# A conditioned transformer block with windowed attention: first modulation from two PSUM banks each, one load for the later modulation columns, a new order on all engines

## The chip, the cores and the metric

The kernel runs on one core of a Trainium2 chip. Five instruction queues work side by side: PE (TensorE, matrix multiplication), DVE (VectorE), ACT (ScalarE), POOL (GpSimd) and SP (SyncE, which here only issues DMA transfers). Each engine takes its own instructions strictly in the order in which the program lists them; between engines there are semaphore waits. The metric is the device time of one execution in microseconds (us), lower is better.

## The reference

One layer: a layer norm whose scale and shift come from a condition vector `c`, attention with a dilated window, a gated residual, and the same again around a two-layer network. All tensors are bf16; S is 2048 tokens, D is 448, there are 16 heads of 28, and F is 1792.

```python
mod = (silu(c) @ w_mod).reshape(1, 6, 1, 448)
sa, ca, ga, sb, cb, gb = (mod[:, i] for i in range(6))
h = layernorm(x) * (1 + ca) + sa
x = x + ga * A(h)              # qkv = h @ wqkv ; window of 8 keys, dilation 2
h = layernorm(x) * (1 + cb) + sb   # ; softmax ; @ wo
x = x + gb * (silu(h @ w1) @ w2)
```

In `A`, token s sees the keys s, s-2, ..., s-14, so even and odd tokens never mix.

## The kernel before

The 2048 tokens are worked in four chunks of 512 (k = 0 to 3), each as 2 x 256 even and odd tokens. Attention runs in nine blocks of about 112 tokens per parity (b = 0 to 8), the two-layer network in the same four chunks. The steps, with the lines of the kernel before:

- `Norm` (L468 to L578) makes the normalized tokens `xn`: statistics by bn_stats on DVE (L480) or by two passes on ACT (L484, L490), a power on POOL (L496), the normalization (L506 to L510). Its result is transposed either on PE, for the first chunk only (`on_pe`, L536, transposes at L546), or by a DMA on SP's queue (`on_dma`, L565, L568). After the transpose the scale and shift of `modc` are applied, the modulation: L552 on ACT or L554 on DVE for the first chunk, L573 or L575 for the others.
- `project` (L639) makes q and k (matmuls at L648, copies out of PSUM at L652) and v (L668, copies at L661). The weights of q and k are first copied into a padded layout (`pad`, L581 to L586, "wp" in the profile).
- `logits` and `values` (L680, L740): q times k at L696, exponent on ACT at L704, mask on DVE at L728, attention times v at L754, normalization on DVE (L759, L760), and a transposing DMA on SP's queue (L764).
- `out_proj` (L775): matmuls at L784, residual add on DVE at L787.
- `ffn1` and `ffn2` (L800, L822): matmuls at L811, silu on ACT at L819, matmuls at L831, residual add on DVE at L836, store at L839.
- The condition: `mod_cols` (L434) makes the scale and shift columns with 32 small matmuls (L444) and copies them into `modc` (L447, L448); `gate` (L454) makes the two gates with four matmuls each (L460), which are then multiplied into the weights (L860, L863).
- `warm_up` (L414) feeds PE with 19 matmuls of no use (7, and six pairs) while the first data are on their way.

Projections use `phases` (L589): each group of 14 matmuls is a "straight" half of 8 and a "crossed" half of 6, which other work may come between.

The order of everything is written out by hand: `ORDER` (L43) lists the numbers of all operations, with the PSUM banks that each takes behind a slash (a "big" number is a pair of banks, a "one" number a single bank) and with v or a where a step can run on DVE or on ACT. `Plan.emit` (L204) emits the instructions in that order, which fixes each engine's queue. The durations, rates and due times beside the operations feed a search for such an order and are not used when `ORDER` is given.

In the first chunk, `on_pe` puts the four transposed 128-column pieces of one half of the tokens (i = 0, 1) into one PSUM bank, and four operations per half modulate one piece each.

The modulation weights `w_mod` lie in `both` and come in eight loads: two for the first norm's columns (issued first on SP), then two each for the first gate, for the second norm, and for the second gate (`load_mod`, L373 and L384).

Of the kernel before, what the change touches and what calls it, by code (L numbers as in the profile page):

```python
# [7 lines left out]
BF16 = mybir.dt.bfloat16  # L8
# [7 lines left out]
D = 448  # L16
H = 16
DH = 28
F = 1792
# [59 lines left out]
def half(j):  # L79
    return slice(K3 * j, K3 * j + K3)  # L80
# [156 lines left out]
def layer(ctx, tc, io, safe):  # L237
# [96 lines left out]
    for r, n in (("big", 3), ("one", 2), ("v", NV), ("p", NP), ("xn", NX), ("o0", 2), ("o1", 2), ("out", len(outb))):  # L334
        P.resource(r, n)
# [631 lines left out]
```

## Time and profile before

| what | value |
|---|---|
| median of three runs | 174.26 us |
| lowest and highest run | 173.8 and 175.14 us |
| the profiled execution's own time | 173.79 us |
| its span, first to last instruction | 172.1 us |
| DVE busy | 101.5 us (59%) |
| ACT busy | 114.7 us (67%) |
| POOL busy | 15.9 us (9%) |
| moved by DMA | 17.48 MB, 102 GB/s in the mean |

The profiled execution took 1.69 us more than its span, and 0.47 us less than the median. Busy time of PE is modelled where matmuls overlap in its pipeline, so a busy PE isn't always a PE at its best pace. The profile also gives the granted clock of PE for any stretch.

### The profile page before, as it was taken

The numbers are of one execution on the slowest core, as the hardware profiler recorded it, in microseconds if no ns is written. First come the engines' busy times: TensorE is split into PE (matmuls) and PEld (weight loads), VectorE is DVE, ScalarE is ACT, GpSimd is POOL, SyncE is SP. The second block draws the span as 40 slices with busy tenths as digits, with TensorE's granted clock in tenths as the row PEclk, the third lists the DMA queues.
The fourth block names the chain that finished last, engine by engine and source line by source line (L and its number), as shares of the span: only waits on it lengthen the run. The fifth ranks groups of instructions, "written<-read, shape, count | busy, mean of one in ns | idle before, by whom it ended". The sixth has DMA issues, their size and how long they took to land.

```text
span 172.1 us, 4285 instructions
## 1 busy us (share of the span) xinstructions
PE 162.7 (95%) x1762; PEld 82.3 (48%) x1763; DVE 101.5 (59%) x261; ACT 114.7 (67%) x162; POOL 15.9 (9%) x38
## 2 busy tenths in 40 slices
PE   7979999699999999999999999999999999999990
PEld 2524444364465455554456555655444454445540
DVE  6889994998798786655578027897662213001031
ACT  3579999786989876789988679653169850473000
POOL 5411230100000130102000000003001100000000
PEclk9999999996999999999999999999999999999999
DMA  5993799943756725021202002224600501000121
GB/s 193 334 363 83 176 231 260 293 116 75 179 155 132 233 65 114 4 47 33 47 27 84 2 0 57 55 55 93 163 29 6 119 0 59 0 0 4 57 84 36
DMA packets 33347, 17.48 MB, mean 102 GB/s; under 512 B 24296, under 2 KB 32936, under 8 KB 33320
## 3 DMA queue, kind: packets, MB, share of 16 engines
q1 hardware_dynamic: 33168, 16.90, 36.9%
q8 instruction: 16, 0.26, 0.7%
q10 hardware_dynamic: 152, 0.23, 0.4%
q14 instruction: 11, 0.09, 0.2%
HBM read 9.12 MB, written 1.84 MB: 64 GB/s over the span
## 4 chain that ended last, share of the span: by engine, by line
PE 72%; DVE 10%; DMA 7%; ACT 6%; issue 2%; DVEq 0%
PE psum L831 25%; PE psum L811 25%; PE psum L648 7%; PE psum L784 7%; PE psum L754 4%; DMA wqk<-xn 3%; PE psum L696 3%; DMA oT<-o 2%; DMA x_all<-in_A_x_dram 2%; PE psum L668 2%; ACT h L552 2%; DVE p L728 1%; DVE st L480 1%; DVE o L760 1%; PE psum L444 1%
## 5 line engine op out<-in xcount | busy, mean ns | idle before, releaser
L831 PE MATMUL psum<-w,both 128*128 128x448 bf16 x224 | 44.7, 353 | 0.0
L811 PE MATMUL psum<-h,w 64*128 64x512 bf16 x392 | 43.6, 376 | 0.0
L704 ACT ACTIVATE p<-psum 128x896 bf16<-128x896 f32 (+1 forms) x36 | 31.8, 931 | 6.2 <-PE psum L696 3.6
L819 ACT ACTIVATE both<-psum 128x1024 bf16<-128x1024 f32 x28 | 27.3, 1021 | 12.7 <-PE psum L811 12.7
L811 PEld LDWEIGHTS <-w 64*128 64x128 bf16 x392 | 20.8, 94 | 20.9 <-issue 0.5
L831 PEld LDWEIGHTS <-both 128*128 128x128 bf16 x224 | 20.8, 98 | 20.0 <-issue 1.2
L836 DVE TENSOR_TENSOR ot<-psum,x_all 128x448 bf16<-128x448 f32 x16 | 9.8, 621 | 27.5 <-PE psum L831 26.3
L496 POOL TENSOR_TENSOR rs<-rs,negh 128x2 f32<-128x2 f32 x16 | 12.6, 790 | 117.6 <-DVE rs L493 117.4
L648 PE MATMUL psum<-h,wp 64*128 64x512 bf16 x168 | 19.8, 377 | 0.1
L728 DVE TENSOR_TENSOR p<-p,maskb 128x1792 bf16<-128x1792 bf16 (+1 forms) x18 | 19.5, 1099 | 0.6 <-ACT p L704 0.4
L648 PEld LDWEIGHTS <-wp 64*128 64x128 bf16 x224 | 10.7, 97 | 13.2 <-issue 1.7
L490 ACT ACTIVATE screp<-x_all,mv 128x448 bf16<-128x448 bf16 x16 | 10.7, 668 | 7.2 <-DVE mv L487 6.9
L784 PE MATMUL psum<-wo,oT 64*128 64x448 bf16 x112 | 12.7, 350 | 0.2 <-DMA oT<-o 0.2
L668 PE MATMUL psum<-wv,h 64*128 64x448 bf16 x98 | 11.8, 350 | 0.9 <-DVE h L554 0.6
L652 ACT CAST qk<-psum 128x1024 bf16<-128x1024 f32 x11 | 10.8, 1004 | 1.8 <-PE psum L648 1.8
L760 DVE TENSOR_TENSOR o<-psum,rc 112x448 bf16<-112x448 f32 (+1 forms) x18 | 11.2, 624 | 0.6
L787 DVE SCALAR_TENSOR_TENSOR x_all<-psum,x_all 128x448 bf16<-128x448 f32 x16 | 9.4, 621 | 2.7 <-PE psum L784 2.0
L754 PEld LDWEIGHTS <-p 128*128 128x128 bf16 x288 | 8.5, 96 | 4.0 <-issue 1.6
L575 DVE TENSOR_SCALAR h<-h,modc 128x512 bf16<-128x512 bf16 x18 | 6.6, 409 | 6.4 <-DMA h<-xn 6.4
L759 DVE RECIPROCAL rc<-psum 112x16 f32<-112x16 f32 (+1 forms) x18 | 4.5, 252 | 9.8 <-PE psum L754 9.8
L754 PE MATMUL psum<-v,p 128*128 128x29 bf16 x288 | 9.6, 176 | 0.4 <-DVE p L728 0.4
L573 ACT ACTIVATE h<-h,modc 128x512 bf16<-128x512 bf16 x6 | 4.7, 808 | 6.9 <-DMA h<-xn 6.9
(84 smaller groups left out, 142.7 us busy)
## 6 DMA issues: line engine op xcount, KB each, us to landing
out_dram<-ot SPq DMA_DIRECT2D x16, 112.0 KB, 1.8
both<-in_w_mod_dram SPq DMA_DIRECT2D x2, 672.0 KB, 4.8
x_all<-in_A_x_dram SPq DMA_DIRECT2D x3, 448.0 KB, 5.9
w<-in_B_w_dram SPq DMA_DIRECT2D x3, 448.0 KB, 4.9
w<-in_B_w_dram SPq DMA_DIRECT2D x1, 896.0 KB, 6.8
both<-in_w_mod_dram SPq DMA_DIRECT2D x2, 336.0 KB, 4.6
w<-in_B_w_dram SPq DMA_DIRECT2D x1, 672.0 KB, 5.5
wv<-in_A_wqkv_dram SPq DMA_DIRECT2D x2, 224.0 KB, 5.6
```

What stands on the lines that cost most here:

```text
L496: G.tensor_tensor(out=rs[:, j:j + n], in0=rs[:, j:j + n], in1=negh[:, 0:n], op=ALU.pow)
L648: return T.matmul(ps[:, j, :], lhsT=w.rearrange("p h d -> p (h d)"), rhs=h[rows, :, t, 128:128 + CP], start=start, stop=stop)
L652: copy_on(o)(out=qk[:, :, g, :, s0:s0 + CP], in_=ps.rearrange("p j (t s) -> p j t s", t=2))
L668: T.matmul(ps[:, par, 0:D], lhsT=h[rows, par, t, b0:b0 + 128], rhs=wv[rows, t, :], start=start, stop=stop)
L704: S.activation(out=out_, in_=ps[:, :, 0:4 * nq].rearrange("p j (g q) -> p j g q", q=nq), func=ACTF.Exp, scale=SCALE)
L728: V.tensor_tensor(out=p, in0=p, in1=maskb[:, 1 if b == 0 else 0, 0:nq].unsqueeze(1).to_broadcast([128, H, nq]), op=ALU.mult)
L754: T.matmul(ps[:, h, 0:DH + 1], lhsT=p[:, at:at + 128], rhs=v[:, h, 0:DH + 1], start=True, stop=True)
L760: V.tensor_tensor(out=box["o"][0:nq, off:off + D].rearrange("p (h d) -> p h d", d=DH), in0=ps[0:nq, :, 0:DH], in1=r.unsqueeze(2).to_broadc ...
L784: T.matmul(ps[par][:, 0:D], lhsT=oT[rows, t, par, s0:s0 + 128], rhs=wo[rows, par, t, :], start=start, stop=stop)
L811: return T.matmul(ps[:, j, :], lhsT=w, rhs=h[rows, :, t, :], start=start, stop=stop)
L819: silus[k].append(P.op(("act", 904.0), lambda o, i=i, box=box: S.activation(out=hid[:, k % 2, :, i, :], in_=box["ps"], func=ACTF.Silu), [m ...
L831: T.matmul(box["ps"][:, 0:D], lhsT=hid[:, k % 2, f % 2, f // 2, 128 * j:128 * j + 128], rhs=w2[:, f // 2 + 7 * (f % 2), :], start=(f == 0) ...
```

## The change

Three things change.

1. In `on_pe`, the four transposed pieces of each half go to two separate PSUM banks, two pieces each. One operation now modulates the two pieces of a bank, on one engine. So each half has two modulation operations where it had four, and the two may run on different engines. In the new order DVE takes the two pieces of the first bank of the first half, and ACT the other six pieces.
2. The columns of `w_mod` for both gates and for the second norm come in one call of `load_mod`: one load of 1344 KB and one of 224 KB in place of three of 336, 672 and 336 KB and three of 56, 112 and 56 KB.
3. `ORDER` is another list: the queues of all engines, the choice between DVE and ACT, and the banks are all new. The planner's counts of banks and its DMA durations are also changed; they only matter to the search that made the list.

```diff
 ORDER = (
-    "75/0 1 0 5 8 2 9 3 4 7 102 6 11 25 84 95 76 79 23 21 94 61 62 63 66 64 82 13 15 14 73 103 85/2 96 97 101 67 69 104 12 80 78 105 98 99v 22 106 100v 86 "
-    "10 88/2 108 107 89 109v 111/3 112 110a 113v 116a 114v 115a 26 161 118/2 119 162 122a 123a 24 77 81 19 20 120v 121a 83 137/2 17 18 124 27 92a 140/3 163 "
...
+    "1 2 53 3 67/0 68 70 0 5 8 6 86 9 11 21 4 10 25 26 54 23 24 87 22 13 7 55 61 62 57 94 95 88 58 93 15 76 77/2 78 59 96 97 66 19 89 90 71 69 12 73 56 "
+    "80/2 91v 103/3/4 92v 98 99 64 104 100 81 101v 102v 74 105v 107/5/2 108 17 18 147 27 148 149 154 63 72 106a 29 109a 60 14 110a 84v 150 151 75 20 16 82a "
...
-    for r, n in (("big", 3), ("one", 2), ("v", NV), ("p", NP), ("xn", NX), ("o0", 2), ("o1", 2), ("out", len(outb))):
+    for r, n in (("big", 2), ("one", 4), ("both", 2), ("v", NV), ("p", NP), ("xn", NX), ("o0", 2), ("o1", 2), ("out", len(outb))):
...
-    ld_mo, ld_mb, ld_m2 = load_mod(2 * D, 3 * D, late), load_mod(3 * D, 5 * D, late), load_mod(5 * D, 6 * D, late)
+    ld_mo = ld_mb = ld_m2 = load_mod(2 * D, 6 * D, late)
...
                     if j == 0:
-                        box["t"] = onet().bitcast(BF16).rearrange("p (k n) -> p k n", k=KT)
+                        for a in range(2):
+                            box[a] = onet().bitcast(BF16)[:, 0:512].rearrange("p (k n) -> p k n", k=2)
                     for k in range(KT):
-                        T.transpose(box["t"][:, k, 128 * j:128 * j + 128], self.box["x"][:, 2 * i + j, 128 * k:128 * k + 128], ident[:])
+                        T.transpose(box[k // 2][:, k % 2, 128 * j:128 * j + 128], self.box["x"][:, 2 * i + j, 128 * k:128 * k + 128], ident[:])
...
-                def mod(o, k, i=i, box=box):
-                    out_, in_ = out_of(k, i), box["t"][:, k, :].rearrange("p (t s) -> p t s", t=2)
-                    scale, shift = modc[:, 1, k:k + 1], modc[:, 0, k:k + 1]
+                def mod(o, a, i=i, box=box):
+                    for k in (2 * a, 2 * a + 1):
+                        out_, in_ = out_of(k, i), box[a][:, k % 2, :].rearrange("p (t s) -> p t s", t=2)
+                        scale, shift = modc[:, 1, k:k + 1], modc[:, 0, k:k + 1]
...
-                d = [P.op(either(455.0, 270.0), lambda o, k=k, mod=mod: mod(o, k), trs + list(waits)) for k in range(KT)]
-                P.op(("none", 0.0), none, d, give=((trs[0], "one"),))
+                d = []
+                for a in range(2):
+                    d.append(P.op(either(910.0, 700.0), lambda o, a=a, mod=mod: mod(o, a), trs + list(waits), take=() if a else ("both",), give=((trs[0], "one"),) + (((d[0], "both"),) if a else ())))
```

What the new order does around the places that the prediction speaks of, engine by engine:

- PE: 9 of the useless matmuls stand before the small matmul on `c` (L429), and 6 between it and the 32 small matmuls of the first norm's columns (11 and 4 before the change). The later matmuls interleave differently; between the first halves of the third chunk's projections stands a run of small matmuls, which now has two attention-times-v steps, the 32 small matmuls of the second norm, one logits step and one more attention-times-v step (before: three, two logits steps and the 32).
- ACT: behind the modulation come one large pad copy (of three; ACT had two and DVE one before), the copy of the 32 tokens that the second chunk shares with the first (on DVE before), the small pad copy (on DVE before), two copies of v, two first passes of statistics for the third chunk (four, for two chunks, before), one copy of q and k, two second passes, another copy of q and k, one modulation of the second chunk, the last copy of q and k of the first chunk, one more first pass, and then the first exponents.
- SP: the two transposing DMAs of the second chunk, then a load of 112 KB, the new loads of 224 and 1344 KB, a load of 56 KB, and the two transposing DMAs of the third chunk, then the loads of `wo`, of a part of `w1` and of `w2`.

More of the change, by code (lines that the diff above doesn't have):

```diff
@@ L219, in emit @@
                 o["at"], o["eng"], o["end"] = got[o["i"]]
-        self.free["one"] = [6, 7]
+        self.free["one"] = [4, 5, 6, 7]
         for o in seq:
@@ L358, in sp, with load @@
         return P.op(("none", land), none, [a], give=((a, "dma"),) + tuple(give)), a
-    def load(kb, out, in_, after=(), rate=0.315):
-        return sp(max(400.0, kb / 0.31), lambda o: nc.sync.dma_start(out=out, in_=in_), [begin] + list(after), 500.0, dma=(470.0, 1300.0, kb / rate))[0]
+    def load(kb, out, in_, after=(), rate=0.36):
+        return sp(max(400.0, kb / 0.31), lambda o: nc.sync.dma_start(out=out, in_=in_), [begin] + list(after), 500.0, dma=(600.0, 1300.0, 150.0 + kb / rate))[0]
     def first_x(i):
@@ new lines, in mod @@
+                def mod(o, a, i=i, box=box):
+                    for k in (2 * a, 2 * a + 1):
+                        out_, in_ = out_of(k, i), box[a][:, k % 2, :].rearrange("p (t s) -> p t s", t=2)
+                        scale, shift = modc[:, 1, k:k + 1], modc[:, 0, k:k + 1]
+                        if o["eng"] == "act":
+                            S.activation(out=out_, in_=in_, func=ACTF.Identity, scale=scale, bias=shift)
+                        else:
+                            V.tensor_scalar(out=out_, in0=in_, scalar1=scale, scalar2=shift, op0=ALU.mult, op1=ALU.add)
@@ L555, in on_pe @@
                 for j in range(2):
                     last = i == 1 and j == 1
-                    trs.append(P.op(("pe", 240.0), lambda o, j=j, tr=tr: tr(o, j), [self.nr[2 * i + j]] + trs[-1:] + (first if i and not j else []), take=() if j else ("one",),
+                    trs.append(P.op(("pe", 240.0), lambda o, j=j, tr=tr: tr(o, j), [self.nr[2 * i + j]] + trs[-1:] + (first if i and not j else []), take=() if j else ("one", "one"),
                                     give=((self.nr[0], "xn"),) if last else ()))
@@ L772, in values @@
             P.later(v_op[bb], [nr])
[L773 removed]
+        trs[b, par] = sp(1250.0, tr, [nr], give=((a, f"o{par}"),), dma=(1215.0, 650.0, 850.0))[0]
     def out_proj(k, i):
```

15 lines of the change are left out of this document (5 added, 10 removed), and 42 rows, old and new, of the table ORDER.

## The prediction

> **What bounds it now.** I read the page first, for the busy shares:
>
> ```profile
> span 172.1 us, 4285 instructions
> ...
> PE 162.7 (95%) x1762; PEld 82.3 (48%) x1763; DVE 101.5 (59%) x261; ACT 114.7 (67%) x162; POOL 15.9 (9%) x38
> ```
>
> PE is busy nearly throughout, and the amount of matrix work is the same after the change. So only time can go that PE spends idle, slowed or on useless work. The table by stretches says where that is (length, busy time of PE, PEld, DVE, ACT and POOL, granted PE clock, DMA share, GB/s):
>
> ```profile
> 10.20:14.44 4.24, 3.39 (x29) 1.31 (x30) 4.04 (x15) 3.76 (x7) 1.00 (x2) 1.00 0.74 242
> 14.44:31.20 16.76, 16.48 (x170) 7.16 (x167) 13.56 (x39) 16.43 (x29) 3.19 (x7) 1.00 0.90 204
> 31.20:36.35 5.15, 3.49 (x45) 1.54 (x44) 5.15 (x9) 3.43 (x5) 0.66 (x1) 1.00 0.63 208
> 36.35:39.66 3.31, 3.27 (x113) 2.82 (x114) 3.19 (x9) 3.09 (x5) 0.00 (x0) 0.94 0.48 126
> 39.66:43.04 3.38, 3.38 (x27) 1.09 (x28) 2.88 (x4) 1.97 (x3) 0.00 (x0) 0.55 0.42 92
> 43.04:56.60 13.56, 13.33 (x238) 7.05 (x242) 11.40 (x24) 12.38 (x16) 0.00 (x0) 1.00 0.64 165
> 56.60:167.70 111.10, 111.08 (x1096) 57.25 (x1095) 53.45 (x135) 69.16 (x93) 6.59 (x8) 1.00 0.21 54
> ```
>
> Behind 56.6 us PE has 111.08 of 111.10 us: nothing to win there, though something to lose. Ahead of it four places matter: the first stretch, where DVE (4.04) and ACT (3.76) are the full ones; the second, where ACT has 16.43 of 16.76; the third, with 1.66 us of idle PE (5.15 less 3.49); and the fifth, where PE is busy at a clock of 0.55.
>
> The timeline of ACT (start, length, line, what; in brackets the idle time before it and what ended it) and three rows of DVE's show the first place:
>
> ```profile
> 9.11 0.56 ACT L552 ACTIVATE h<-psum,modc 128x256 bf16<-128x256 bf16 x1 [0.32 <-DVE h L554]
> 10.16 1.48 ACT L552 ACTIVATE h<-psum,modc 128x256 bf16<-128x256 bf16 x3 [0.48 <-DVE h L554]
> 12.11 0.56 ACT L552 ACTIVATE h<-psum,modc 128x256 bf16<-128x256 bf16 x1 [0.48 <-DVE h L554]
> 12.58 1.76 ACT L583 COPY wp<-wqk 128x896 bf16<-128x896 bf16 x2
> 14.24 1.71 ACT L661 CAST v<-psum 128x896 bf16<-128x896 f32 x2
> ...
> 17.95 0.58 ACT L484 ACTIVATE both<-x_all 128x448 bf16<-128x448 bf16 x1
> 18.44 0.18 ACT L484 ACTIVATION_READ_ACCUMULATOR both<-x_all 128x1 f32 x1
> 18.53 0.99 ACT L652 CAST qk<-psum 128x1024 bf16<-128x1024 f32 x1
> 19.42 0.81 ACT L573 ACTIVATE h<-h,modc 128x512 bf16<-128x512 bf16 x1
> 20.14 0.65 ACT L490 ACTIVATE both<-x_all,mv 128x448 bf16<-128x448 bf16 x1
> 20.70 0.19 ACT L490 ACTIVATION_READ_ACCUMULATOR both<-x_all,mv 128x1 f32 x1
> ...
> 24.30 1.28 ACT L704 ACT_TABLE_LOAD   x1
> 25.59 1.94 ACT L704 ACTIVATE p<-psum 128x1024 bf16<-128x1024 f32 x2
> ```
>
> ```profile
> 8.35 0.41 DVE L508 TENSOR_SCALAR xn<-x_all,mv,rs 128x512 bf16<-128x512 bf16 x1
> 8.67 0.41 DVE L554 TENSOR_SCALAR h<-psum,modc 128x256 bf16<-128x256 bf16 x1
> 9.71 0.41 DVE L554 TENSOR_SCALAR h<-psum,modc 128x256 bf16<-128x256 bf16 x1 [0.63 <-ACT h L552]
> ```
>
> DVE and ACT take turns on one bank: each stands idle until the other is through. And PE's timeline gives its pace:
>
> ```profile
> 1.26 4.45 PE L416 MATMUL psum<-both 128*128 128x512 bf16 x11 [1.26 <-DVE both L311]
> 5.69 0.17 PE L429 MATMUL psum<-ident,sc 4*128 4x4 bf16 x1
> 5.79 1.04 PE L416 MATMUL psum<-both 128*128 128x512 bf16 x4
> 6.67 0.22 PE L444 MATMUL psum<-scT,both 128*128 128x1 bf16 x3
> 7.24 0.86 PE L444 MATMUL psum<-scT,both 128*128 128x1 bf16 x29 [0.35 <-DVE xn L508]
> ...
> 14.44 8.82 PE L648 MATMUL psum<-h,wp 64*128 64x512 bf16 x78
> ...
> 39.66 3.38 PE L648 MATMUL psum<-wqk,wp 64*128 64x512 bf16 x16
> ...
> 43.28 1.47 PE L648 MATMUL psum<-wqk,wp 64*128 64x512 bf16 x12
> ```
>
> **The separate banks.** In the new program ACT's first modulation waits for the transposes and the columns alone, not for DVE. The columns come when they came: the 29 matmuls of L444 start at 7.24, when the weights' second load is there (the first three had run, and the fourth is the first to need it), and end at 8.10; copies on DVE until about 8.5. DVE's last two normalizations come next (0.32 each, from the start at 8.35 to that at 8.67), so its two modulations, at 0.41, end at 9.95; ACT's two of the first half, at 1.48 / 3 = 0.49, run beside them from about 8.9 to 9.95. Before, the fourth of them ended at 10.65 (10.16 + 0.49). The second half is ACT's alone: 9.95 + 4 x 0.49 = 11.9, where the last ended at 12.67 before. That is 0.75 us. The padded weights follow: one large copy (1.76 / 2, less overlap: 0.83), the shared tokens' copy (256 columns as in L552: 0.49), the small pad (half a large one: 0.45) end at 13.7 on ACT; DVE's two large ones are through by 13.1. V of blocks 0 and 1 hides in front. So the projections of q and k start at about 13.7, not 14.44: **0.75 us earlier**.
>
> A price may stand against this: PE now reaches the small matmul on `c` after 9 useless ones, at 1.26 + 9 x 0.40 = 4.9, and stands idle until 5.69. The six behind it, at 0.26, end at about 7.2, just when the weights land, so I take it at nothing. It costs 6 x (0.40 - 0.26) = 0.8 us if the idle time puts off the faster pace, and can't be a gain.
>
> **ACT's queue up to the first exponents.** Steps by the rows above (start to start where the next follows at once): first pass 0.70, second pass 0.78, copy of q and k 0.90, copy of v 0.85, modulation 0.72, table 1.29. Behind 13.7: 2 x 0.85 + 2 x 0.70 + 0.90 + 2 x 0.78 + 0.90 + 0.72 + 0.90 = 8.1, so the last copy of the first chunk's q and k ends at 21.8. PE needs four groups and a half by then, 64 matmuls at 8.82 / 78 = 0.113: 7.2 us, ready at 20.9. It then waits for that modulation and the copy, and starts the first logits at 22.0. Before, the same 64 matmuls were through at 14.44 + 7.2 = 21.7 with no such wait. So the gain of 0.75 is eaten here, and **0.3 us** besides.
>
> But the exponents start at 21.8 + 0.6 + 1.29 = 23.7, where they started at 25.59: 1.9 us earlier, because two first passes, a second pass and copies of the second chunk went behind them. The later waits of PE hang on those (banks freed by exponents, masks behind exponents). In the third stretch and its run-up PE was idle for 1.66 + 0.28 = 1.94 us. Following the new queues on through this part in the same way, I find PE waiting 0.25 and 0.1 (banks held by block 0's first exponents), 0.5 (block 1's logits behind a copy of q and k on ACT) and 0.35 (block 2's logits behind an exponent). That is 1.2, so 0.75 saved. The order also puts one logits step of block 2, 16 small matmuls, ahead of the first attention-times-v step; at the 3.31 / 113 = 0.029 of the fourth stretch that is 0.45 of work that was behind it. Net: -0.3 + 0.75 + 0.45 = **0.9 us ahead** at the point that was 36.35.
>
> **The slow clock.** The 16 matmuls at 39.66 took 3.38 us, though 12 of the same shape took 1.47 at 43.28; at 0.113 they need 1.8. So **1.6 us** were lost to a clock of 0.55 over that stretch. What stood in front was 3.31 us of the smallest matmuls (113 in the row), preceded by a wait. In the new order that run is shorter by those 16 and a part step (96 matmuls, 2.8 us), with full-size projections on both sides and no wait that I can find in it, so I take the 1.6 us as gained. The Trainium skill ("TensorE: Matmul & The Clock Gate", Part 1, The HAM clock gate) speaks against counting on it: activity is judged in free-running windows of 3.4 us that don't restart with the kernel, so whether a quiet run throttles is luck of phase, in the old kernel and in the new. The row's length of 3.38 agrees; that the phase shifts between runs is shown by no run here. By that rule the sum would be the rival's below.
>
> **From 43.04 to 56.60.** The new queues give PE four waits: 0.4 (block 3's logits behind a copy of q and k on DVE), 0.3 and 0.25 (block 4's logits, block 3's second mask), 0.2 (the second output projection behind block 1's transposing DMA). Together 1.15; before, it was idle 0.23 here. So up to 0.9 is lost. But the copies and masks that it would wait for start earlier too, most of them by the 1.9 us of the exponents. I take 0.3 lost, between 0.9 lost and 0.2 gained (the idle 0.23). **Behind 56.6** I find each norm, silu and exponent ahead of PE by at least 0.5 us; 0. The end is the same: 14 matmuls of L831, an add, a store.
>
> **The one load.** The gates' weights are 1344 KB at once, with 224 + 112 + 56 KB around them, from about 17.3. At the second stretch's 204 GB/s these 1736 KB take 8.5 us, to 25.8; at the 126 of a later row 13.8, to 31.1. The first gate's turn on PE comes at about 29.6. Nothing at the likelier rate, which is that of the same time; 1.5 us lost at the other end. SP issues four transfers fewer, which shortens a queue that nobody waits for there.
>
> **Sum.** 0.9 + 1.6 - 0.3 + 0 = 2.2 us off the profiled execution: 173.79 - 2.2 = 171.6. The median lies 0.47 above that execution, so about 172.0 for the median. The unknown terms reach 0.5 below (the third term at +0.2) and 0.8 or 0.6 above: the forecast's own range is 171.3 to 172.9.
>
> **Rivals.** First, *the slow clock is no difference*: the new order meets it too, or the timed runs of before mostly lack it. Then 0.6 is left: 173.6. For it speaks that such a run of small matmuls is still there, 2.8 us of it; against it, that before needed 3.3 us and a wait to show it, and that the timed runs (173.8 to 175.14) lie no lower than the profiled one that had it. Chance 0.2.
>
> Second, *the change doesn't part the engines*: DVE and ACT still take turns, by a wait that I overlook, or the idle time before `c` is paid. The modulation then ends 0.75 to 0.8 later, and all behind it: 172.8. The waits of the program speak against it. 0.08.
>
> Third, *slower, by the third chunk's transposes*. They stand on SP behind the one large load, and share the DMA engines with it:
>
> ```profile
> wqk<-xn SPq DMA_TRANSPOSE x2, 5.3
> ```
>
> They took 5.3 us already, beside the smaller loads. Now the second is issued, by the same walk along the queues, at about 24.2 and would land at 29.5. Its four modulations stand on DVE behind the masks of block 0, which end at 30.4, and PE comes to that chunk's first projection at 32.8. Up to a landing at 31.2 it costs nothing. If the packets of 1344 KB are served in front of it at the 126 GB/s of the later row, it starts at 31.1 and lands at 36.4: 5.2 us of PE, in order, with all behind it, and 172.0 + 5.2 = 177.2. It decides from a landing at 33.4 (31.2 + 2.2, the gain gone), and from 35.2 the kernel is slower by 1%. That the row of 204 GB/s already holds transposes beside loads speaks against it. 0.16.
>
> **Chances.** Forecast 0.56, rivals 0.2, 0.08 and 0.16. About 1% is what a measurement of this kernel can tell from no change; here that is 172.5 and 176.0 around the median of 174.26. Of the forecast's range the part up to 172.5 is faster, some four fifths: 0.45. The rest of it and the first two rivals, at 172.8 and 173.6, are within 1%: 0.11 + 0.28 = 0.39. Slower: 0.16. The range runs from 170.8 (the lower end, less the 0.5 that the timed runs of before spread below their median) to 174.4 (the first rival with the 0.8 for the wait on `c`), and leaves out the third rival.
>
> **What would show it.** In the new profile: the last L554 row at about 11.9 (no idle "<-DVE" between its rows); PE's projections of q and k from 13.7; a wait of PE before its first logits at 22; the first exponent at 23.7; no stretch with a clock under 0.9 behind 10 us; the same work of PE about 2.2 us earlier at the fourth chunk's projections. I am wrong if PE waits at the first gate, if DVE waits for the third chunk's transposes beyond 31 us, if the slow clock is back, or if PE is idle behind 56.6.

## The result and the profile after

| kernel | median, us (executions) | lowest to highest, us |
|---|---|---|
| before | 174.36 (6) | 173.42 to 175.14 |
| changed | 172.11 (6) | 171.42 to 174.06 |

The ratio is 0.9864, with a 95% interval from 0.9817 to 0.9911: 1.4% faster, or 2.25 us by the medians. Ratios, here and below, leave out executions more than 1.5% above the fastest of their kernel, which in the second batch of the experiments takes out most executions of before that met a slow clock; so they need not equal the quotient of the medians. The forecast was 172.0. That this is so close is partly luck, as the terms of the sum show: the profiled execution of the changed kernel took 172.53 us, only 1.26 less than the profiled one of before, and several terms missed and partly made up for one another.

The page of the changed kernel (span, busy times, granted clock of PE in 40 slices):

```profile
span 170.8 us, 4278 instructions
...
PE 161.5 (95%) x1763; PEld 78.8 (46%) x1763; DVE 102.9 (60%) x260; ACT 112.9 (66%) x163; POOL 14.7 (9%) x38
...
PEclk9999999999999999999999999999999999999998
```

The slice with a clock of 0.6 in the middle is gone (the 0.8 at the end lies behind the last matmul). For the rest, the table by stretches is divided at three points where PE has done the same work in both kernels: the first projection of q and k, the 16 matmuls of the third chunk's projections behind the run of small ones, and the 12 that follow with one logits step between; then on to the last residual add. The columns are length, busy time and count of PE, PEld, DVE, ACT and POOL, clock, DMA share, GB/s. Before:

```profile
14.44:39.66 25.22, 23.24 (x325) 11.52 (x322) 21.91 (x55) 22.95 (x37) 3.85 (x7) 0.99 0.79 195
39.66:43.28 3.62, 3.62 (x37) 1.24 (x34) 2.88 (x4) 1.97 (x3) 0.00 (x0) 0.58 0.46 103
43.28:167.72 124.44, 124.17 (x1321) 64.15 (x1313) 64.85 (x158) 81.54 (x108) 6.59 (x8) 1.00 0.26 65
```

The same three of the changed kernel:

```profile
14.76:38.31 23.55, 22.91 (x325) 10.85 (x322) 22.36 (x56) 23.46 (x39) 3.82 (x6) 1.00 0.75 202
38.31:40.45 2.14, 2.14 (x36) 0.91 (x34) 2.06 (x5) 2.02 (x3) 0.00 (x0) 1.00 0.32 61
40.45:166.11 125.66, 123.98 (x1321) 61.63 (x1313) 67.31 (x160) 80.01 (x107) 5.91 (x8) 1.00 0.29 68
```

The counts of PE agree (325, 1321; one record is missing in the middle), so lengths can be subtracted. The start is 0.32 **later** (14.76 against 14.44). The next part is 1.67 shorter, the slow part 1.48 shorter, the long rest 1.22 **longer**. Together 1.61 less at the last add; behind it 0.3 of that is lost again in the last stores. So the changed kernel won three microseconds and gave back one and a half, in two places. The rows of PE name both:

```profile
1.26 4.02 PE L416 MATMUL psum<-both 128*128 128x512 bf16 x9 [1.26 <-DVE both L311]
6.23 0.18 PE L429 MATMUL psum<-ident,sc 4*128 4x4 bf16 x1 [0.95 <-ACT sc L424]
6.34 2.74 PE L416 MATMUL psum<-both 128*128 128x512 bf16 x6
8.88 1.02 PE L444 MATMUL psum<-scT,both 128*128 128x1 bf16 x32
...
14.76 7.37 PE L651 MATMUL psum<-h,wp 64*128 64x512 bf16 x64
22.63 0.40 PE L699 MATMUL psum<-qk 28*128 28x128 bf16 x16 [0.51 <-ACT qk L655]
...
38.31 1.90 PE L651 MATMUL psum<-wqk,wp 64*128 64x512 bf16 x16
...
47.94 0.55 PE L757 MATMUL psum<-v,p 128*128 128x29 bf16 x16 [1.46 <-DVE o L763]
```

(The lines of this part stand 2 or 3 further down than before: L554 and L556 are the first chunk's modulation on ACT and DVE, L576 and L578 that of the later chunks, L651 is the projection of q and k, L664 the copy of v, L699 the logits, L731 the mask, L757 attention times v, L763 its normalization.)

First place: PE comes to the matmul on `c` (L429) after 9 useless matmuls and stands idle for 0.95, and the six behind it take 2.74, 0.46 each, where before they took 0.26: PE was still at its slow pace at 9 us. Second place: at 47.9 a wait of 1.46 that the old order did not have.

Most of the 1.67 won in between has a name too. In the old order DVE stood for 2.13 ahead of the third chunk's modulation, until its transposing DMA had landed. A copy of v (L661) stood queued behind that modulation, though its matmuls had ended at 29.6, and PE waited 1.31 for the copy. DVE and PE before:

```profile
30.51 0.41 DVE L575 TENSOR_SCALAR wqk<-wqk,modc 128x512 bf16<-128x512 bf16 x1 [2.13 <-DMA wqk<-xn]
...
31.55 1.08 DVE L661 CAST v<-psum 128x896 bf16<-128x896 f32 x1
```

```profile
32.69 0.37 PE L696 MATMUL psum<-qk 28*128 28x112 bf16 x14 [1.31 <-DVE v L661]
```

In the new order DVE makes two masks first and comes to that modulation when the DMA has landed, with no wait:

```profile
28.84 2.35 DVE L731 TENSOR_TENSOR p<-p,maskb 128x2048 bf16<-128x2048 bf16 x2
31.11 0.41 DVE L578 TENSOR_SCALAR wqk<-wqk,modc 128x512 bf16<-128x512 bf16 x1
```

So the new order took one wait of this kind away and, as the part on the wait at 47.9 shows, put another in.

The modulation itself was parted as the change says. ACT's and DVE's rows:

```profile
10.40 2.84 ACT L554 ACTIVATE h<-psum,modc 128x256 bf16<-128x256 bf16 x6 [3.13 <-PE psum L547]
```

```profile
10.72 0.72 DVE L556 TENSOR_SCALAR h<-psum,modc 128x256 bf16<-128x256 bf16 x2
```

ACT does its six pieces in one block, with no idle time "<-DVE" inside, and DVE's two lie beside it. The block is right; it only begins 1.5 us later than forecast (10.40 against about 8.9).

### The profile page after: what moved, and what is told of

The parts are those of the page before. It is cut to its first block, busy times and chain, and to the rows that moved or that the text cites. A ratio compares the mean times of both kernels' runs of the same rounds, so it can differ in the third digit from the quotient of the medians.

```text
span 170.8 us, 4278 instructions
## 1 busy us (share of the span) xinstructions
PE 161.5 (95%) x1763; PEld 78.8 (46%) x1763; DVE 102.9 (60%) x260; ACT 112.9 (66%) x163; POOL 14.7 (9%) x38
## 3 DMA queue, kind: packets, MB, share of 16 engines
HBM read 9.12 MB, written 1.84 MB: 64 GB/s over the span
## 5 line engine op out<-in xcount | busy, mean ns | idle before, releaser
L814 PEld LDWEIGHTS <-w 64*128 64x128 bf16 x392 | 18.9, 94 | 22.7 <-issue 0.4
L496 POOL TENSOR_TENSOR rs<-rs,negh 128x2 f32<-128x2 f32 x16 | 11.7, 731 | 119.8 <-DVE rs L493 82.0
L651 PE MATMUL psum<-h,wp 64*128 64x512 bf16 x168 | 20.0, 377 | 0.1
L731 DVE TENSOR_TENSOR p<-p,maskb 128x1792 bf16<-128x1792 bf16 (+1 forms) x18 | 19.5, 1100 | 0.9 <-ACT p L707 0.9
L651 PEld LDWEIGHTS <-wp 64*128 64x128 bf16 x224 | 10.3, 94 | 12.9 <-PE psum L651 1.1
L490 ACT ACTIVATE screp<-x_all,mv 128x448 bf16<-128x448 bf16 x16 | 10.7, 667 | 4.2 <-DVE mv L487 4.0
L763 DVE TENSOR_TENSOR o<-psum,rc 112x448 bf16<-112x448 f32 (+1 forms) x18 | 11.2, 625 | 0.6
L578 DVE TENSOR_SCALAR h<-h,modc 128x512 bf16<-128x512 bf16 x18 | 6.7, 409 | 7.5 <-DMA h<-xn 7.5
L757 PE MATMUL psum<-v,p 128*128 128x29 bf16 x288 | 9.5, 176 | 1.6 <-DVE o L763 1.5
L757 PEld LDWEIGHTS <-p 128*128 128x128 bf16 x288 | 8.4, 96 | 4.8 <-issue 2.7
L416 PE MATMUL psum<-both 128*128 128x512 bf16 x19 | 8.0, 578 | 1.3 <-DVE both L311 1.3
L655 ACT CAST qk<-psum 128x1024 bf16<-128x1024 f32 x9 | 9.0, 1003 | 0.1
```

What stands on the lines that cost most here:

```text
L490: S.activation(out=scratch, in_=x_all[:, us[j], :], func=ACTF.Square, bias=mv[:, j, 0:1], scale=ROOT, accum_out=mv[:, j, 1:2])
L496: G.tensor_tensor(out=rs[:, j:j + n], in0=rs[:, j:j + n], in1=negh[:, 0:n], op=ALU.pow)
L651: return T.matmul(ps[:, j, :], lhsT=w.rearrange("p h d -> p (h d)"), rhs=h[rows, :, t, 128:128 + CP], start=start, stop=stop)
L731: V.tensor_tensor(out=p, in0=p, in1=maskb[:, 1 if b == 0 else 0, 0:nq].unsqueeze(1).to_broadcast([128, H, nq]), op=ALU.mult)
L757: T.matmul(ps[:, h, 0:DH + 1], lhsT=p[:, at:at + 128], rhs=v[:, h, 0:DH + 1], start=True, stop=True)
L763: V.tensor_tensor(out=box["o"][0:nq, off:off + D].rearrange("p (h d) -> p h d", d=DH), in0=ps[0:nq, :, 0:DH], in1=r.unsqueeze(2).to_broadc ...
```

## The experiments

Every run also timed the kernel before on the same chip; the executions of before are shared by the runs of one batch (three batches, four runs each in the order of the table, with medians of before of 174.24, 173.57 and 173.94; one execution of before in the second took 323.96 us). "Ratio" is to those, with its 95% interval.

| run | median, us (executions) | ratio to before |
|---|---|---|
| after_again | 172.74 (12) | 0.9918 (0.9880 to 0.9956) |
| c_after_11 | 172.22 (6) | 0.9889 (0.9831 to 0.9946) |
| late_mod_behind_norm | 170.73 (6) | 0.9834 (0.9779 to 0.9889) |
| one_bank | 173.33 (12) | 0.9953 (0.9913 to 0.9994) |
| loads_split | 171.53 (12) | 0.9935 (0.9896 to 0.9973) |
| old_order_two_banks | 172.24 (6) | 0.9898 (0.9833 to 0.9963) |
| old_order_dense_run | 173.84 (12) | 1.0010 (0.9969 to 1.0051) |
| c_after_11_late_mod | 170.37 (6) | 0.9835 (0.9779 to 0.9892) |
| after_third | 172.29 (11) | 0.9906 (0.9864 to 0.9948) |
| late_mod_again | 170.32 (6) | 0.9817 (0.9760 to 0.9873) |
| late_mod_c_after_13 | 170.26 (6) | 0.9791 (0.9747 to 0.9836) |
| old_order_c_after_9 | 174.31 (12) | 0.9994 (0.9951 to 1.0038) |

### The start: when `c` comes, and when PE gets fast

The changed kernel was run twice more, unchanged, and once with two of the useless matmuls moved ahead of the one on `c` (operation 71 in `ORDER`: 11 ahead and 4 behind, as before the change).

> The changed kernel once more, to see what differs between its own executions. If PE's faster clock at the start is put off by the idle time ahead of the matmul on c (0.95 us in the first profile) in every execution, its profile shows again 6 matmuls of 512 columns at 0.45 us behind that matmul and the first projection of q and k at about 14.7 us, and the runs stay near 172.1. If it is the luck of the clock's window, this profile may show them at 0.22 to 0.26 and the projection at about 13.9, about 0.9 us less in all (171.5).

> The changed kernel once more, beside the next three on one chip, to have its own spread next to theirs. Both theories: 171.5 to 172.8 us in the median, and executions of two kinds, some 1 us apart: with the fast clock from about 4 to 6 us in the profile (projections of q and k from 13.8) or from about 9 to 10 (projections from 14.8 to 15.3).

> The changed kernel with one pair of useless matmuls moved from behind the small matmul on c to the front of it (11 and 4, as before the change). Theory 1, the wait on c puts off the fast clock: idle time ahead of that matmul falls from 0.95 to 0 or 0.3 us, the four behind run at about 0.26 us, the first projection of q and k starts at 13.7 to 14.0 and the median falls by 0.5 to 0.9 us against the changed kernel. Theory 2, the window's phase decides whatever stands there: no difference in the median over the runs (within 0.3 us), and slow starts in both.

```diff
-    "1 2 53 3 67/0 68 70 0 5 8 ...
+    "1 2 53 3 67/0 68 70 71 0 5 8 ...
-    ... 66 19 89 90 71 69 12 73 56 "
+    ... 66 19 89 90 69 12 73 56 "
```

after_again starts as the first profile did: the six useless matmuls behind `c` take 2.74 again. The profiled execution of after_third, the same program, has quite another start. Its PE rows:

```profile
5.44 0.17 PE L429 MATMUL psum<-ident,sc 4*128 4x4 bf16 x1 [0.40 <-ACT sc L424]
5.54 1.47 PE L416 MATMUL psum<-both 128*128 128x512 bf16 x6
6.85 0.94 PE L444 MATMUL psum<-scT,both 128*128 128x1 bf16 x32
...
12.66 1.68 PE L651 MATMUL psum<-h,wp 64*128 64x512 bf16 x14
```

The six useless matmuls take 0.245 each and the projections start at 12.66, 2.1 us earlier than in the first profile of the very same program. Two things differ. `c` arrives when it likes: the silu on it (L424), which waits for that load, starts between 5.08 and 6.34 in the fourteen profiled executions. And the fast pace begins at another time. With the start of that silu as zero, the profiled executions fall into groups:

| order, banks | pace of the matmuls behind `c` | silu on `c`, us | projections, us | between |
|---|---|---|---|---|
| old, one bank a half (before, old_order_c_after_9, old_order_dense_run) | fast | 5.32, 6.00, 5.97 | 14.44, 15.06, 14.60 | 9.12, 9.06, 8.63 |
| old, two banks (old_order_two_banks) | fast | 5.88 | 13.60 | 7.72 |
| new, two banks (after_third, late_mod_again, loads_split, late_mod_behind_norm, c_after_11, late_mod_c_after_13, c_after_11_late_mod) | fast | 5.08, 5.42, 6.14, 6.18, 6.24, 6.30, 6.34 | 12.66, 13.00, 13.73, 13.77, 13.77, 13.86, 13.88 | 7.53 to 7.59 |
| new, two banks (changed kernel, after_again) | slow | 5.86, 6.33 | 14.76, 15.24 | 8.90, 8.91 |
| new, one bank (one_bank) | slow | 6.23 | 15.82 | 9.59 |

So three things set the start: the arrival of `c` (1.3 us of scatter), the banks, and the pace (1.3 us: 8.90 against 7.58). The banks are worth 0.9 in the old order (7.72 against the 8.63 of old_order_dense_run) and 0.7 in the new one (8.90 against 9.59). The other two of the old order are no measure of them: 9.12 holds a pause of 0.35 within the 32 small matmuls, and 9.06 two more useless matmuls behind `c`. The forecast counted only the banks.

Why the pace? The trace records when the granted clock changes, and all these times lie on a grid of 3.41 us whose phase differs from execution to execution. The two windows of that length ahead of the fast pace in the first profile of the changed kernel, which begins at 9.44 (the clock column shows 1.00 where the trace holds no record yet, so the pace is read from the matmuls):

```profile
2.62:6.03 3.41, 2.66 (x7) 0.65 (x5) 2.93 (x15) 1.60 (x4) 0.87 (x8) 1.00 0.97 318
6.03:9.44 3.41, 3.21 (x27) 1.55 (x28) 1.47 (x8) 0.96 (x4) 1.59 (x6) 1.00 1.02 363
```

And those of c_after_11_late_mod (its edit is below), in which the window ends at nearly the same time, 6.01, but PE, with 11 useless matmuls, had work until then:

```profile
2.60:6.01 3.41, 3.41 (x9) 0.97 (x7) 2.84 (x15) 1.45 (x3) 0.78 (x8) 1.00 1.03 362
6.01:9.42 3.41, 2.78 (x47) 1.84 (x47) 1.87 (x11) 1.18 (x5) 1.70 (x6) 1.00 1.08 362
```

With 2.66 of 3.41 busy the fast pace waited for another whole window; with 3.41 of 3.41 it came at 6.01. Windows with 2.94 and 3.19 us of busy PE (late_mod_behind_norm, late_mod_again) also released it at once; those of after_again and one_bank, with 2.00 and 2.24, did not. In all fourteen profiles the fast pace begins at the end of the first window with 2.94 us or more of busy PE. So the idle time ahead of `c` costs nothing if the window's end falls ahead of it or soon after its begin, and 1.3 us otherwise (seen with 0.95 to 1.41 us of it). The Trainium skill ("TensorE: Matmul & The Clock Gate", Part 1, The HAM clock gate) says that the clock is released after a busy window of about 3.4 us of a free-running monitor, and that the number of slow matmuls therefore differs between runs of one kernel; the traces agree, with 3.41 us and a fast pace from 4.23 at the earliest to 10.20 at the latest.

c_after_11 itself did not take the idle time away: in its execution `c` came at 6.24 and the fast pace already at 4.23, so PE was idle for 1.34 all the same. 172.22 against 172.74 settles nothing.

The last batch tried it with 13 ahead of `c` and 2 behind, on top of the edit of late_mod_again (next part), and the reverse in the old order, 9 and 6.

> late_mod_again with 13 of the useless matmuls ahead of the small one on c and 2 behind (9 and 6 before), so that PE has work until c is there. Theory (the idle 1 to 1.4 us ahead of c, where it falls into the clock's first window, holds back the fast clock by one window of 3.4 us and the projections by 1.0 to 1.5): idle ahead of c under 0.7, fast clock by 7.5 us at the latest, projections from 13.7 to 14.1, and a median 0.2 to 0.6 us below late_mod_again, its slowest executions 1 us below that one's slowest. Rival (the clock starts by the phase alone, whatever PE does ahead of c): the same median within 0.2, and the same spread.

> The kernel before with 9 useless matmuls ahead of the small one on c and 6 behind (11 and 4 before), nothing else. Theory of the idle time: 0.2 to 0.6 us above the kernel before in the median, idle ahead of c of 0.9 to 1.4 us. Rival: no difference.

```diff
-    "1 2 53 3 67/0 68 70 0 5 8 ...
+    "1 2 53 3 67/0 68 70 71 69 0 5 8 ...
-    ... 66 19 89 90 71 69 12 73 56 "
+    ... 66 19 89 90 12 73 56 "
```

With 13 ahead PE's idle time is gone, its fast pace begins at 6.40 and the projections at 13.86 with `c` at 6.30. But the median is the same (170.26 against 170.32): the forecast gain of 0.2 to 0.6 did not come. Only the slowest of six executions is lower, 171.03 against 171.83. The trace shows why there is little to gain at the fast pace: the useless matmuls behind `c` do not set the start then. In the new order ACT's second pass of the first chunk's statistics (L490) stands behind its copy of the transposed `c` (L431), and DVE's normalization hangs on that pass. DVE in late_mod_c_after_13:

```profile
7.76 0.17 DVE L493 TENSOR_SCALAR rs<-mv 128x2 f32<-128x2 f32 x1 [1.29 <-ACT both L490]
```

The 32 small matmuls end at 8.18 there, and DVE comes to the copy of their result (L447) at 9.04, behind steps of that normalization. So from `c` to the projections it takes 7.53 to 7.59 with 2, 4 or 6 useless matmuls behind `c`; having more of them ahead can only guard against the slow pace.

In the old order, 9 ahead made no difference that can be told (174.31 against 173.94, ratio 0.9994); there the profiled execution had its fast pace from 5.26. So the price of the idle time is shown in the traces where it falls. How often it falls, the times only hint at: of the 29 executions of the changed kernel 24 have a mean granted clock over 0.9915, and these fall apart into nine from 170.72 to 171.68 and fifteen from 172.22 to 173.25. The profile with the fast start is one of the nine, the two with the slow start are among the fifteen; the start of the others is not on record.

### The banks

one_bank is the changed kernel with both operations of a half reading one bank again (everything else as it is); old_order_two_banks is the kernel before with two banks a half and nothing else.

```diff
+                        one = onet().bitcast(BF16).rearrange("p (k n) -> p k n", k=KT)
                         for a in range(2):
-                            box[a] = onet().bitcast(BF16)[:, 0:512].rearrange("p (k n) -> p k n", k=2)
+                            box[a] = one[:, 2 * a:2 * a + 2, :]
```

> The changed kernel with the four transposed pieces of a half in one bank again, the order unchanged. Theory 1, DVE and ACT take turns on one bank: the first half's two modulations of ACT come behind DVE's two and end about 0.7 us later, and since ACT alone does the rest, the last modulation and the first projection of q and k come about 0.7 us later; the end 0.3 to 0.7 us later, as part of it is lost in later waits. Theory 2, the order alone brings the gain: within 0.2 us of the changed kernel.

> The kernel before with the separate banks alone: two banks for each half, its order and its split of the eight modulations between DVE and ACT unchanged. Theory 1, the banks make the engines take turns: the idle times of 0.3 to 0.6 us between the modulations go, the last modulation ends at about 11.3 instead of 12.67 us, the first projection of q and k starts 0.7 to 1.2 us earlier, and the end comes 0.3 to 1.0 us earlier, since ACT's queue behind it is what it was. Theory 2, the gain of the changed kernel is the order's: the modulation ends earlier, but the end moves by under 0.3 us.

one_bank takes 0.6 us more than after_again (173.33 against 172.74, both with 12 executions of one batch, which overlap: 172.52 to 174.46 and 171.14 to 174.32). Its ACT and DVE rows show the turns:

```profile
11.91 2.84 ACT L555 ACTIVATE h<-psum,modc 128x256 bf16<-128x256 bf16 x6 [4.28 <-DVE h L557]
```

```profile
11.09 0.72 DVE L557 TENSOR_SCALAR h<-psum,modc 128x256 bf16<-128x256 bf16 x2
```

ACT's block of six now begins 0.82 behind DVE's two pieces, when these are through, though it reads other columns; in the changed kernel it began 0.32 ahead of them (10.40 against 10.72). PE pays for it: the 28 matmuls of v take 3.99 (3.30 in after_again), and q and k start at 15.82, 0.6 later than in after_again, both at the slow pace and with `c` at 6.23 and 6.33. At the 12 matmuls of the third chunk it is 1.0 behind (41.96 against 40.93), and 0.5 of that comes back at the wait near 48, which is 0.84 there and 1.32 in after_again.

old_order_two_banks is the other direction. Its rows of ACT and DVE at this place show the turns of the first half gone, and one left in the second, where DVE and ACT still share a bank:

```profile
8.92 1.91 ACT L553 ACTIVATE h<-psum,modc 128x256 bf16<-128x256 bf16 x4
11.27 0.56 ACT L553 ACTIVATE h<-psum,modc 128x256 bf16<-128x256 bf16 x1 [0.44 <-DVE h L555]
```

```profile
8.74 0.72 DVE L555 TENSOR_SCALAR h<-psum,modc 128x256 bf16<-128x256 bf16 x2
```

Its projections start at 13.60 with `c` at 5.88. The time, 172.24 against 173.57, is 1.3 us below before by the medians and 1.8 by the ratio, with an interval of 0.6 to 2.9. So the banks alone bring a good part of the gain in the old order. Whether it is all of it six executions can't tell: on the same chip loads_split, which is the changed kernel but for its loads, has a median of 171.53.

### The slow clock

The executions of the kernel before are of two kinds. In the three batches 13 of 23, 12 of 23 and 11 of 22 executions have a mean granted clock under 0.9915 (one window of 3.41 us at half clock in 172 takes off 0.0099); the median of the others is 173.3, 172.8 and 173.3, which is 1.4 to 1.9 below that of the first kind. So the slow clock that the profile of before shows is met by about half of its executions. old_order_dense_run breaks the run of small matmuls (the quiet run of the expectation below) up, with six useless full-size ones ahead of the 32 of the second norm:

```diff
-            ps[0] = onet()[:, 0:2 * KT].rearrange("p (a k) -> p a k", a=2)
+            bank = onet()
+            for _ in range(6 if dst0 else 0):
+                T.matmul(bank[:, 0:D], lhsT=wv[:, 0, 0:128], rhs=wv[:, 1, :], start=True, stop=True)
+            ps[0] = bank[:, 0:2 * KT].rearrange("p (a k) -> p a k", a=2)
```

> The kernel before with six useless matmuls of 448 columns in front of the 32 small ones of the second norm, in the middle of the quiet run at 36 to 39.7 us. They cost 6 x 0.19 = 1.1 us of PE. Theory 1, the quiet run is what lets the clock fall: no execution has a mean clock near 0.99 any more (13 of 23 have it in the kernel before, at 174.2 to 175.5 us; the other 10 lie at 172.8 to 173.9), and all lie near 173.3 + 1.1 = 174.4. Theory 2, the fall has another cause (a reaction to heat or to the load before): half of the executions still have it, and the median lies 1.1 us above that of before, near 175.4.

None of its 12 executions had the low clock, against 12 of 23 of the kernel before on the same chip. Its rows show what they cost and what they save:

```profile
37.51 1.31 PE L441 MATMUL psum<-wv 128*128 128x448 bf16 x6
...
40.75 1.90 PE L651 MATMUL psum<-wqk,wp 64*128 64x512 bf16 x16
```

The 16 matmuls behind the run take 1.90 as in the changed kernel, not 3.38. As 1.31 is paid always and 1.6 saved half the time, nothing is left (ratio 1.0010). The median of 173.84 lies under the 174.4 of the first theory, but fits it on this chip, where the quick kind of before has 172.8. And the cause is shown: it is the run of small matmuls. old_order_two_banks, which keeps that run, has the slow window; the window in front of it and the slow one:

```profile
35.52:38.93 3.41, 3.16 (x112) 2.74 (x112) 3.34 (x10) 3.19 (x5) 0.00 (x0) 1.00 0.47 123
38.93:42.34 3.41, 3.41 (x22) 1.10 (x18) 2.95 (x5) 2.09 (x3) 0.00 (x0) 0.50 0.45 102
```

PE counts as busy for 3.16 of 3.41 there, more than the 2.94 that released the clock at the start: with the small shapes (128x29, 28x112, 128x1) the modelled busy time is no measure of what the clock follows. The reverse is seen too: a window of after_third (42.21 to 45.62) with only 2.19 us of busy PE in 58 matmuls, ten of them of 512 columns, kept the full clock. In the changed kernel and its variants with the new order 12 of 83 executions lie under 0.9915 (before and the two old-order variants that keep the quiet run: 46 of 86), and none of their profiles has the slow window. The run of small matmuls is only 2.5 us long there (35.82 to 38.31), so a window holds at least 0.9 us of other work beside it. That seems to make the fall rarer but need not rule it out: in old_order_c_after_9 a window with eight full-size matmuls at its start (35.98 to 39.39) was still followed by one at half clock. Where those 12 lost their clock isn't on record, and not all need have lost time in the middle: a halved clock behind the last matmul lowers the mean as well (0.992 in the profile of late_mod_behind_norm, at 170.55 us).

### The wait at 47.9

The changed kernel's DVE and SP around it:

```profile
46.64 0.41 DVE L578 TENSOR_SCALAR h<-h,modc 128x512 bf16<-128x512 bf16 x1 [1.75 <-DMA h<-xn]
46.97 0.25 DVE L762 RECIPROCAL rc<-psum 112x16 f32<-112x16 f32 x1
47.26 0.62 DVE L763 TENSOR_TENSOR o<-psum,rc 112x448 bf16<-112x448 f32 x1
```

```profile
40.56 2.60 SPq L571 DMA_TRANSPOSE h<-xn  x2
```

DVE's queue puts the fourth chunk's modulation ahead of a normalization of block 2. The modulation needs the transposing DMA that SP issues from 40.56 on and that lands at 46.6, so DVE stands for 1.75 us with the normalization queued behind it, whose operands are there from 45.4 at the latest (its 32 matmuls at L757 start at 44.45 and take 0.97); PE needs the bank that the normalization frees, and loses 1.46. The edit puts three modulations of that chunk (256 and 257 on DVE, 259 on ACT) behind those normalizations:

```diff
-    ... 219/2 309 39 256v 52 332/6 45 259a 324/7 333 310 335 349/0/1 "
-    "350 220 257v 325 326 383 315/6 221a 228/0 ...
+    ... 219/2 309 39 52 332/6 45 324/7 333 310 335 349/0/1 "
+    "350 220 325 326 383 256v 257v 315/6 221a 259a 228/0 ...
```

> The changed kernel with the modulations of the fourth chunk moved back in the queues of DVE (two, behind the normalizations of block 2) and ACT (one, behind block 3's first exponent and a copy of q and k). Theory 1, PE's wait of 1.46 us at 47.9 is the wait of DVE for the transposing DMA, with the normalization of block 2 queued behind it: the wait goes, and 1.0 to 1.5 us with it, if nothing else is late next: the ratio to before falls by about 0.007. Theory 2, the normalization is late by itself or the banks are held by ACT: the wait stays above 0.8 us and the median moves by under 0.4.

> The changed kernel with both edits: 11 useless matmuls ahead of the one on c, and the fourth chunk's modulations behind the normalizations of block 2. If the two work at places that don't touch, the median is that of the second alone (170.7) less what the first brings (0.3 to 0.7): 170.0 to 170.6. If the first only depends on the clock's window, 170.7 within 0.3.

> The fourth chunk's two first modulations moved behind block 2's normalizations on DVE and ACT's queues, as in the earlier run of it. Theory (the wait of 1.46 us at 47.9 is a loss of its own, passed on to the end): 1.2 to 1.6 us less than after_third in the median, and PE's longest wait behind 15 us is 0.4 to 0.5. Rival (the gain of the earlier run came from its early fast clock, 5.75 us): within 0.5 us of after_third.

The rows of PE in late_mod_again at the same work:

```profile
44.67 0.56 PE L757 MATMUL psum<-v,p 128*128 128x29 bf16 x16
45.17 2.84 PE L671 MATMUL psum<-wv,wqk 64*128 64x448 bf16 x28
...
49.60 0.57 PE L757 MATMUL psum<-v,p 128*128 128x29 bf16 x17 [0.42 <-ACT v L664]
```

The wait is gone, and 0.42 is late next, behind a copy of v. On one chip: 170.32 against 172.29 for the changed kernel (after_third); the ratio to before falls from 0.9906 to 0.9817, though the intervals still overlap. Part of the 2.0 is chance, as the wait can give only 1.46 - 0.42 = 1.04, but all four runs with this edit lie between 170.26 and 170.73. The profiles free the gain from the scatter of the start: from the 12 matmuls of the third chunk to the last group of three residual adds on DVE, the four with the edit take 121.4 to 121.5, and the five without it that have two banks and the new order 122.4 to 122.9. So 1.0 to 1.5 us is the edit's. c_after_11_late_mod, at 170.37, lies between its two forecasts and decides nothing. The edit together with 13 useless matmuls ahead of `c` is the fastest found: 0.9791 (0.9747 to 0.9836).

### The one load

loads_split makes three loads each of the two, at the same place in SP's queue.

```diff
-    ld_mo = ld_mb = ld_m2 = load_mod(2 * D, 6 * D, late)
+    cuts = ((2 * D, 3 * D), (3 * D, 5 * D), (5 * D, 6 * D))
+    ld_mo = ld_mb = ld_m2 = [
...
```

> The changed kernel with the one load of 1344 KB as three again (336, 672, 336 KB) and the one of 224 KB as three (56, 112, 56 KB), at the same place in SP's queue and waited for together. Theory 1, the merging is worth nothing: PE doesn't wait at the first gate in either, SP's queue has some 4 us of slack before the next transposing DMA; the median within 0.3 us of the changed kernel (172.1 to 172.7). Theory 2, one load is better for the DMA engines: the last of the three lands over 1 us later than the one load, the third chunk's transposes with it, and the kernel is 0.5 us slower or more.

171.53 with a ratio of 0.9935, against 0.9906 and 0.9918 for the two repeats of the changed kernel: no difference that can be told. (The median lies 0.6 below the forecast 172.1 to 172.7, on a chip where before is 0.7 lower than in the first batch.) Its transposing DMAs of the third chunk land in 4.3 us, not later than with the one load (4.6). In the changed kernel PE comes to both gates without a wait. The third chunk's transposing DMAs, the subject of the rival on the slow side, land sooner than before (4.6 against 5.3 in the median), and DVE, which waited 2.13 for them before, doesn't wait. The changed kernel, KB and median us from issue to landing:

```profile
both<-in_w_mod_dram SPq DMA_DIRECT2D x1, 1344.0 KB, 7.2
...
wqk<-xn SPq DMA_TRANSPOSE x2, 4.6
```

## Why the prediction was right, and where it was not

**The separate banks: right in mechanism, and about right in size.** 0.75 was taken; from the arrival of `c` the traces give 0.9 in the old order and 0.7 in the new, and the times 0.6 (one_bank) to 1.3 (old_order_two_banks). The start of the projections was less well placed: behind a `c` as early as in the profile of before (5.32) and at the fast pace, the table gives 5.32 + 7.58 = 12.9, where the working has 13.7.

**The price on `c`: wrong.** It was taken at nothing, with 0.8 as the bound. In the profile it ate the gain of the banks and 0.32 more: 0.54 by a later `c` (5.86 against 5.32), which has nothing to do with the change, and 1.3 by the pace. The step that failed is "the six behind it, at 0.26": they took 0.46 in two of the changed kernel's three profiles, and 0.245 in the third. (At 0.26 they would have ended at 5.79 + 1.56 = 7.35, a little behind the 7.24 of the weights, not at 7.2.)

**ACT's queue up to the first exponents: too careful, and with the wrong cause.** Between the projections and the third chunk's 16 matmuls 0.15 was forecast (0.9 less the 0.75) and 1.67 came. The 0.45 in it, for a logits step done earlier, is no gain at that point, since PE does the same 325 matmuls up to there in either order; without it the working gives 0.3 lost. PE's wait ahead of the first logits was forecast from 20.9 to 22.0 and is 0.51; of the further waits of 1.2 none is there: PE is idle for 23.55 - 22.91 = 0.64 in that stretch, against 1.98 before. The working hung the old idle time on the exponents. The rows of before put 1.31 of it down to a copy of v behind a modulation that waited for its DMA, and that wait is what went. The first exponent is at 24.46, 0.8 behind the forecast 23.7, with projections that start 1.1 behind theirs.

**The slow clock: right in the profile, half right for the median.** 1.6 forecast, 1.48 measured between the two profiled executions. But the sum set it against a median as if every execution of before had it; half do. On average it is worth about (46/86 - 12/83) x 1.6 = 0.6. The first rival described this; it is true of about half the executions of before.

**From 43.04 on: wrong in size and place.** 0.3 lost was taken from four waits with a bound of 0.9; 1.22 was lost, by one wait that was not among the four. The DVE queue was followed for masks and copies, and the modulation's DMA was passed over: its landing, 4.7 us behind the later of the two issues, is what counts. It is the same oversight as in the stretch before: there too a modulation's DMA held DVE.

**The one load and behind 56.6: right**, both nothing. PE needs 111.11 us for its last 1096 matmuls up to the last add, and needed 111.12.

Of the signs named: ACT's block without turns, the wait at 22, the missing slow clock and the idle-free rest behind 56.6 came; the projections from 13.7 and the first exponent at 23.7 came 1.1 and 0.8 late; the third chunk's later projections were 2.8 us earlier (40.45 against 43.28), but of this 1.6 was left by the fourth chunk's last (64.37 against 65.95), where 2.2 was forecast. The forecast of 172.0 held by luck in its parts. The terms that were too good (slow clock, start, the wait at 47.9: 0.1, 1.1 and 0.9 us, and 0.3 in the last stores) stand against one that was too careful (1.5), which leaves the profiled execution 0.9 above the 171.6 forecast for it. The median came out right because the working put it 0.47 above the profiled execution, and it lies 0.42 below. That most of the timed executions started better than the profiled one would explain it, but their starts are not on record. The stated range of 171.3 to 172.9 is also wider at its lower end than the terms named for it, which give 172.0 - 0.5 = 171.5.

## What to carry to other kernels

Follow each in-order queue past every instruction that waits for a DMA, and ask what stands behind it that is ready: here one modulation put ahead of one normalization cost 1.5 us of the busiest engine, and the old order had lost 1.3 us to the like. Two engines that read different columns of one PSUM bank still take turns, if the program orders them by the bank; giving each its own bank was worth 0.7 to 0.9 us at the start of the projections here. Before a gain is counted, ask how many executions show the loss: a slow clock in one profile was there in half of them.

## What the runs showed of the hardware

- The granted clock changes on a grid of 3.41 us (in the profile of before at 5.14, 39.27 and 42.68) whose phase differs from one execution to the next; the fast pace of one and the same program began at 4.66, 9.44 and 10.20 us.
- A window with 2.66 us of busy PE out of 3.41 did not release the clock, one with 2.94 did; and 3.16 us of busy PE in 112 matmuls, nearly all of the smallest shapes, halved it for the next window, while 2.19 us in 58, ten of them of 512 columns, did not.
- The load of `c`, 1 KB in two transfers at one and the same place of ACT's queue, scattered over 1.3 us: the silu that waits for it began between 5.08 and 6.34.
